# An adaLN transformer block on one core: order of the front loads, of block 1's norm chain and of the last W_o products, with re-chosen plan constants

## The chip, the cores and the metric

The kernel runs on one core of one Trainium2 chip. The metric is device time in microseconds (us); the time before is the median of three runs, 764.05 us (761.28 to 764.38). TensorE multiplies matrices into PSUM (eight banks of 128 x 512 fp32), ScalarE and VectorE read PSUM and write SBUF, GpSimd works on SBUF alone, and transfers are issued from SyncE's queue (SP) and a few from ScalarE's.

## What is computed

One transformer block over 2048 tokens of width 512, 32 heads of 16, hidden width 1376, with the modulation vectors computed from one condition vector c:

```python
mod = (_silu(c) @ w_mod).reshape(c.shape[0], 6, 1, -1)          # sa, ca, ga, sb, cb, gb
h = _layernorm(x) * (1 + ca) + sa
q, k, v = split(h @ wqkv)                                       # 32 heads of 16
o = softmax(q @ k.T * 16 ** -0.5) @ v
x = x + ga * (o @ wo)
h = _layernorm(x) * (1 + cb) + sb
x = x + gb * (gelu(h @ w1 + b1) @ w2 + b2)
```

## The kernel before

Work is cut into four blocks of 512 tokens. Token block b of x lies in tile xb[b]; the normalised and modulated block, transposed, in hT. kT holds the keys, VE the values (with a column of ones per head, which gives the softmax's sum), qm the queries. A *query group* qi (32 of them) is one block of 512 queries with four heads; its 16 key tiles kt hold 128 keys each; a *row* is one head of the four. Scores of a row are one matmul (`qk`, line 807), 128 keys by 512 queries in one bank; the product with the values is one matmul (`pv_issue`, line 963) into O.

Exponentials are made in two ways. ScalarE takes units of two rows (128 x 1024, line 1148, into pA or pB; the two alternate, five buffers each). For some key tiles, named in DKT, VectorE and GpSimd do it: VectorE makes an int16 whose bits, read as a float, approximate a power of two (a *pass*, line 1219, one per row), and then three *shifts* of the whole tile, each an addition of a constant (line 1190 on VectorE, 1196 on GpSimd); these four versions are multiplied with VE and with three scaled copies of it, VV, and their sum is a better exponential. `fill` (line 978) issues matmuls with zeros where TensorE would stand idle.

The **front** (lines 183 to 382) is written in order by hand. c and W_m0 (the first third of w_mod, 1 MB) are loaded from ScalarE's queue; SP issues xb[0] in two halves, then W_k, W_q, xb[1], W_v, xb[2], xb[3], W_m1, and later W_m2 and W_o. VectorE takes `ln_stats` of the four token tiles of xb[0] (line 256), two aggregates after each pair, GpSimd the inverse root (266, 267), VectorE the norm (271); TensorE transposes (275), runs two filler matmuls (`warm`, 234), and then multiplies W_m0 with silu(c) (281), from which hT of block 0 (290 on ScalarE, 293 on VectorE), the first keys and the first queries follow.

From there to the end of attention a **planner** written in Python sets the order. It keeps a clock for each engine (T), asks the engine that is free first what it can do next (`pe`, `act`, `dve`, `pool`), and emits that instruction; the costs it reckons with are constants (EXP_BUSY, PASS_BUSY, the `busy` of each task, `out` as the delay until the result can be used). So a constant changes no instruction by itself, but the order of the instructions on each queue. *Jobs* are matmul groups in a PSUM bank with an evacuation, *tasks* are single instructions on another engine; each has a gate (the position in the list of query groups from which it may be taken) and things that must be done before it. `add_ln1(b)` makes the tasks of the norm of block b: four statistics `st`, an aggregate `ag`, the root `rt` on GpSimd, four norms `nm`, and then transposes (on TensorE for block 1, by DMA for blocks 2 and 3, line 452) and hT; its gate is 0.001 b. `add_k` and `add_v` make the keys (kT, copied at 301 or 303) and the values. Two constants name the part of a gate in which a tail job is spread: U_GATE for the up-projection, OUT_GATE for the down-projection. VectorE's policy is one line:

```python
if o_copy(now) or do_evac(now, DV) or recip(now) or p_pass(now) or do_task(now, DV):
```

so a task is looked at only when no bank waits to be evacuated. GpSimd takes a shift when VectorE has at least POOL_MIN us of open work. The order of the scores is: for key tiles 0 to 3 query groups 0 and 1, then key tiles 4 to 7, and so on for these two groups; from group 2 on, group after group. So ScalarE can do 16 units before it needs the keys of block 1.

After the planner, **`last_tail`** (from line 1410) finishes the last token block by hand: VectorE copies O out (1426), four matmuls pick the sums (1430), VectorE inverts them (1432) and spreads them (1439), four matmuls transpose them (1441), VectorE scales O (1445), and for each of the four token tiles the products with W_o are completed: `outer` adds x and three head groups, `last_ch` the first half of the fourth, the last `plain` (W_z[:, 1]) its second half. Three tiles had their `outer` part as planner jobs; the fourth's stands here. Statistics (1465), norm, transposes, up-projection, gelu, down-projection and the stores follow.

Of the kernel before, what the change touches and what calls it, by code (L numbers as in the profile page):

```python
# [23 lines left out]
D = 512  # L24
# [4 lines left out]
NQB = 4  # L29
# [10 lines left out]
DKT = (3, 7, 11, 13, 14, 15)  # L40
# [10 lines left out]
INF = 1e18  # L51
# [27 lines left out]
U_GATE = (2.0, 4.8)  # L79
# [6 lines left out]
POOL_MIN = 0.9  # L86
# [5 lines left out]
Z_AHEAD = 3  # L92
Z_GATE = 0.35
# [50 lines left out]
def adaln_block(ctx: ExitStack, tc: tile.TileContext, A_x, A_wqkv, A_wo, B_x, B_w1, B_b1, B_w2, B_b2,  # L144
# [28 lines left out]

    def load_mod(i, eng):
        t = prom.tile([P, NC, 2 * D], BF16, name="W_m")
        eng.dma_start(out=t, in_=wm_v[:, :, 2 * i * D:2 * (i + 1) * D])
        return t
# [9 lines left out]
    nc.sync.dma_start(out=W_k, in_=wqkv_v[:, :, D:2 * D])  # L187
    nc.sync.dma_start(out=W_q, in_=wqkv_v[:, :, 0:D])
    nc.sync.dma_start(out=xb[1], in_=x_tok[1])
    nc.sync.dma_start(out=W_v, in_=wqkv_v[:, :, 2 * D:3 * D])  # L190
    for b in range(2, NQB):
        nc.sync.dma_start(out=xb[b], in_=x_tok[b])
    W_m1 = load_mod(1, nc.sync)
# [138 lines left out]

    st0 = small.tile([P, 4, 6], FP32, name="st")
    roots = []
    warm(WARM[0])
    for h in range(2):
        for t in (2 * h, 2 * h + 1):
            ln_stats(xb[0], st0, t)
        mv = ln_aggr(st0[:, 2 * h:2 * h + 2, :], 2)
        roots.append((mv, ln_root(mv, 2)))  # L340
# [10 lines left out]
    norm_pair(0)  # L351
    silu_c()
# [101 lines left out]
    def add_ln1(b):  # L454
# [6 lines left out]
        for t in range(4):  # L461
            task(("st", b, t), g, [("x", b)] + ([("st", b, t - 1)] if t else []), DV, 0.64, lambda t=t: stats(t))
        task(("ag", b), g, [("st", b, 3)], DV, 0.6, lambda: lnst[b].append(ln_aggr(lnst[b][0], 4)))
        task(("rt", b), g, [("ag", b)], PO, 1.35, lambda: lnst[b].append(ln_root(lnst[b][1], 4)))
        for t in range(4):
            task(("nm", b, t), g, [("rt", b)] + ([("nm", b, t - 1)] if t else []), DV, 0.36,
                 lambda t=t: ln_norm(xb[b], xb[b], lnst[b][1], lnst[b][2], t, t))
# [363 lines left out]
    def d_next(now, avoid):  # L831
        if dcur[0] is None:
# [6 lines left out]
            if left < 3:  # L839
                return None  # L840
# [270 lines left out]
    def do_task(now, e):  # L1111
        p = pos()
# [205 lines left out]
    def dve(now):  # L1318
        if o_copy(now) or do_evac(now, DV) or recip(now) or p_pass(now) or do_task(now, DV):
            return True  # L1320
        return hold[0] <= now + 0.03 and emit_shift(DV, now)
# [88 lines left out]
    def last_tail():  # L1410
# [22 lines left out]
        for tt in range(len(pz), 4):  # L1433
            for fn in outer(bank(po[tt]), tt):
                fn()
            last_ch(tt)
# [11 lines left out]
        for tt in range(4):  # L1448
            plain(bank(po[tt]), otl[:, tt * P:(tt + 1) * P], W_z[:, 1, :], False, True)
        warm(12, kw)  # L1450
# [219 lines left out]
```

## Time and profile before

| what | value |
|---|---|
| median of three runs | 764.05 us (761.28 to 764.38) |
| profiled execution: its time / its span | 764.2 us / 762.4 us |
| ScalarE: busy, share of the span | 719.1 us, 94% |
| TensorE: busy, share (fillers included) | 740.0 us, 97% |
| VectorE / GpSimd busy | 689.1 us, 90% / 436.9 us, 57% |
| exponentials on ScalarE | 730 of 128 x 1024, mean 1065 ns |
| VectorE passes / shifts | 588, mean 681 ns / 243, mean 758 ns |
| GpSimd shifts | 198, mean 1898 ns |
| mean granted clock of TensorE | 0.993 |

How to read it: times within the span count from its start. In the timeline a row has the start, the length, engine, line, operation, result and operands, the number of instructions merged into it, and in brackets how long the engine stood idle before it and what released it. Busy times of neighbouring instructions overlap (an exponential takes 1065 ns in the mean, but the next starts some 905 ns after it in an undisturbed run), so the start-to-start distance is what one instruction costs in a full queue. PE is TensorE, PEld its weight load, DVE VectorE, ACT ScalarE, POOL GpSimd.

### The profile page before, as it was taken

Reading aid. Unit: us, or ns where it says so; the run is one execution under the profiler, and the core shown is the slowest. Engines: PE = TensorE matmul, PEld = TensorE weight load, DVE = VectorE, ACT = ScalarE, POOL = GpSimd, SP = SyncE. Lnnn points to the kernel's source line nnn. Section 1 sums busy time; section 2 is a strip of 40 time slices with the busy share of each in tenths; the row PEclk is TensorE's granted clock in tenths of the full one; section 3 lists DMA queues with packets and bytes.
Section 4 is the critical chain, followed back from the end, with each engine's and each line's share of the span. In section 5 each row is a group of like instructions: output and inputs, shape, how many; then the busy total and the mean of one; then the engine's idle time right before and its main releaser. Section 6 shows DMA issues by size and latency. Waiting matters only on the chain.

```text
span 762.4 us, 21212 instructions
## 1 busy us (share of the span) xinstructions
PE 740.0 (97%) x8608; PEld 227.9 (30%) x8608; DVE 689.1 (90%) x1194; ACT 719.1 (94%) x776; POOL 436.9 (57%) x277
## 2 busy tenths in 40 slices
PE   7999999999999999999999999999999999999998
PEld 3322322232222222222222222222232222222255
DVE  5867989999999999999999999999999999999962
ACT  2799999999999999999999999999999999999953
POOL 3201686786568556577558567556667566636610
PEclk9899999999999999999999999999999999999999
DMA  9410100042200200000100200000100200001100
GB/s 314 114 16 2 25 2 18 10 109 67 38 17 3 51 5 16 9 24 24 44 17 3 49 4 17 9 25 24 44 17 10 37 9 17 9 17 30 52 2 31
DMA packets 45969, 25.39 MB, mean 33 GB/s; under 512 B 30973, under 2 KB 40674, under 8 KB 45866
## 3 DMA queue, kind: packets, MB, share of 16 engines
q1 hardware_dynamic: 44906, 22.74, 11.9%
q8 instruction: 69, 1.13, 0.6%
q10 hardware_dynamic: 960, 1.25, 0.5%
q14 instruction: 34, 0.28, 0.1%
HBM read 16.74 MB, written 2.64 MB: 25 GB/s over the span
## 4 chain that ended last, share of the span: by engine, by line
PE 58%; ACT 29%; issue 6%; DVE 4%; DMA 2%; POOL 1%; SPq 1%; ACTq 0%; POOLq 0%; DVEq 0%
PE PS L963 20%; PE PS L807 20%; ACT pB L1148 14%; ACT pA L1148 13%; PE PS L229 13%; PE PS L622 3%; DVE t L1219 2%; DVE t L1190 1%; ACT uG L681 1%; DMA W_m<-in_w_mod_dram 1%; PE PS L978 1%; POOL t L1196 1%; DMA h2T<-uG 0%; SPq L1259 0%; ACT L1148 0%
## 5 line engine op out<-in xcount | busy, mean ns | idle before, releaser
L1196 POOL TENSOR_SCALAR t<-t 128x2048 int16<-128x2048 int16 x198 | 374.2, 1898 | 246.2 <-DVE t L1190 133.6
L1219 DVE TENSOR_SCALAR t<-PS 128x512 int16<-128x512 f32 x588 | 377.5, 681 | 25.8 <-PE PS L807 21.9
L1148 ACT ACTIVATE pA<-PS 128x1024 bf16<-128x1024 f32 x365 | 388.6, 1065 | 4.7 <-PE PS L807 4.4
L1148 ACT ACTIVATE pB<-PS 128x1024 bf16<-128x1024 f32 x365 | 388.9, 1065 | 1.7 <-PE PS L807 0.9
L807 PE MATMUL PS<-qm,kT 32*128 32x512 bf16 x2048 | 303.1, 383 | 6.7 <-ACT pB L1148 2.6
L963 PE MATMUL PS<-t,VV 128*32 128x512 f16 x1764 | 224.5, 384 | 6.2 <-POOL t L1196 3.3
L1190 DVE TENSOR_SCALAR t<-t 128x2048 int16<-128x2048 int16 x243 | 176.5, 758 | 0.5
L807 PEld LDWEIGHTS <-kT 32*128 32x128 bf16 x2048 | 83.9, 91 | 295.8 <-issue 293.9
L963 PE MATMUL PS<-pA,VE 128*32 128x512 bf16 x730 | 169.6, 388 | 0.0
L963 PE MATMUL PS<-pB,VE 128*32 128x512 bf16 x730 | 164.1, 389 | 0.0
L963 PE MATMUL PS<-t,VE 128*32 128x512 f16 x588 | 142.0, 385 | 0.0
L963 PEld LDWEIGHTS <-VE 128*32 128x32 bf16 x2048 | 60.3, 94 | 81.3 <-issue 76.3
L963 PEld LDWEIGHTS <-VV 128*32 128x32 bf16 x1764 | 58.8, 94 | 64.1 <-issue 56.1
L229 PE MATMUL PS<-h2T,W 128*32 128x512 bf16 x528 | 41.7, 383 | 0.9 <-DMA h2T<-uG 0.8
L229 PE MATMUL PS<-W,uG 128*32 128x512 bf16 x528 | 41.5, 383 | 0.0
L978 PE MATMUL PS<-hT,zeros 128*32 128x512 bf16 x360 | 34.4, 387 | 0.0
L1295 POOL TENSOR_TENSOR OT<-o_sb,rb 128x512 bf16<-128x512 f32 x16 | 20.3, 1271 | 12.0 <-DVE t L1190 10.2
L310 DVE TENSOR_SCALAR qm<-PS,qmask 128x512 bf16<-128x512 f32 x32 | 22.7, 741 | 3.7 <-PE PS L229 3.4
L673 DVE TENSOR_SCALAR uG<-PS,b1c 128x512 bf16<-128x512 f32 x33 | 24.5, 743 | 1.5 <-PE PS L229 1.2
L266 POOL TENSOR_SCALAR rs<-mv 128x4 f32<-128x4 f32 (+1 forms) x10 | 4.3, 431 | 31.6 <-DVE mv L261 31.2
L229 PE MATMUL PS<-hT,W_k 128*32 128x512 bf16 x256 | 21.4, 410 | 0.9 <-DVE hT L293 0.9
L229 PE MATMUL PS<-hT,W_q 128*32 128x512 bf16 x256 | 21.6, 399 | 0.0
(128 smaller groups left out, 377.8 us busy)
## 6 DMA issues: line engine op xcount, KB each, us to landing
rb<-d SPq DMA_DIRECT2D x120, 32.0 KB
W_m<-in_w_mod_dram SPq DMA_DIRECT2D x2, 1024.0 KB
xr<-in_A_x_dram SPq DMA_DIRECT2D x4, 512.0 KB
o_sb<-o SPq DMA_DIRECT2D x60, 32.0 KB
out_dram<-ob SPq DMA_DIRECT2D x14, 128.0 KB
xb<-in_A_x_dram SPq DMA_DIRECT2D x3, 512.0 KB
W<-in_B_w_dram SPq DMA_DIRECT2D x4, 344.0 KB
W<-in_B_w_dram SPq DMA_DIRECT2D x5, 256.0 KB
```

The costliest lines, as they stand in the source:

```text
L229: nc.tensor.matmul(out=ps[32 * g:32 * g + 32, :], lhsT=lhsT[:, 32 * g:32 * g + 32], rhs=rhs, start=start, stop=stop)
L310: nc.vector.tensor_scalar(out=qm[(b, ch)][:, par, :], in0=ps, scalar1=qmask[:, par:par + 1], scalar2=None, op0=ALU.mult)
L622: nc.tensor.matmul(out=ps, lhsT=lhsT, rhs=rhs, start=start, stop=stop)
L673: nc.vector.tensor_scalar(out=X["u"][:, fc, :], in0=bank(ps), scalar1=late["b1c"][:, fc:fc + 1], scalar2=None, op0=ALU.add)
L807: nc.tensor.matmul(out=dst, lhsT=kT[32 * r:32 * r + 32, ch, kt * P:(kt + 1) * P], rhs=qm[(b, ch)][32 * r:32 * r + 32, par, :], start=True, ...
L963: nc.tensor.matmul(out=bank(O[qi])[32 * r:32 * r + 32, :], lhsT=w, rhs=rhs, start=(n == 1), stop=last)
L978: nc.tensor.matmul(out=bank(O[qi])[32 * r:32 * r + 32, :], lhsT=zeros[:, 0:32], rhs=hT[:, r, 0:512], start=False, stop=False)
L1148: nc.scalar.activation(out=t[:, 0:n, :], in_=PS[:, b0:b0 + n, :], func=ACT.Exp, scale=math.log(2.0) / STEP)
L1190: nc.vector.tensor_scalar(out=t16[:, rs, :], in0=d["tile"][:, rs, :], scalar1=float(MJ[j]), scalar2=None, op0=ALU.add)
L1196: nc.gpsimd.tensor_scalar(out=t16[:, rs, :], in0=d["tile"][:, rs, :], scalar1=1.0, scalar2=float(MJ[j]), op0=ALU.mult, op1=ALU.add)
L1219: nc.vector.tensor_scalar(out=d["tile"][:, r:r + n, :], in0=PS[:, i:i + n, :], scalar1=T_BIAS, scalar2=0.0, op0=ALU.add, op1=ALU.max)
L1295: nc.gpsimd.tensor_tensor(out=ot, in0=o, in1=rb, op=ALU.mult)
```

## The change

Front loads: W_k, W_q, xb[1], W_v, xb[2] and xb[3] are put in a list. After the first statistic of xb[0], W_k is issued with a dependency on that VectorE instruction, and W_q behind it; after the fourth, xb[1] with a dependency on it, and the others behind it. W_m1 is issued after the first `norm_pair`. Block 1's chain: while fewer than 32 score tiles are taken, VectorE looks first for a task with a gate up to 0.0015, that is, block 1's statistics, aggregate and norms. The plan's cost of a statistic is 0.61 instead of 0.64, and statistics and norms have no delay (`out=0.0`). The last tail: the last products of tiles 0 and 1 now stand ahead of the fourth tile's `outer` and `last_ch`, those of tiles 2 and 3 behind them, and ten fillers follow instead of twelve. Four constants are others; D_END only names the 3 that stood in the code.

```diff
@@ -37,7 +37,7 @@
 TURNS = {}
 TURN = 2
-DKT = (3, 7, 11, 13, 14, 15)
+DKT = (2, 3, 7, 13, 14, 15)
 NV = 4
 STEP = 1024.0
@@ -76,20 +76,22 @@
 K_GATE = (-1.8, 0.4)
 Q_GATE = -0.9
 X1_GATE = (0.3, 1.3)
-U_GATE = (2.0, 4.8)
+U_GATE = (1.7, 5.0)
 OUT_GATE = (4.6, 7.8)
 OPEN_N = 12
 DMA_T = 4.0
 LN1_DMA = (2, 3)
 LN2_DMA = True
 D_PEND = 3
-POOL_MIN = 0.9
+POOL_MIN = 1.0
 D_WAIT = 0.6
 WHY = False
 TIE = True
 SEARCH = None
 NARROW = False
 Z_AHEAD = 3
+LOAD_AT = (0, 3)
+D_END = 3
 Z_GATE = 0.35
@@ -171,6 +173,18 @@
     wqkv_v = A_wqkv.rearrange("(j p) n -> p j n", p=P)
     wo_v = A_wo.rearrange("(c p) n -> p c n", p=P)
+    def load_next(dst, src, after=None):
+        n0 = len(nc.cur_bb.bb.instructions)
+        nc.sync.dma_start(out=dst, in_=src)
+        if after is not None:
+            mine = [i for i in nc.cur_bb.bb.instructions[n0:] if i.engine == nc.sync.engine]
+            tc.add_manual_dep(mine[0], after.name,
+                              mybir.DependencyInfo(mybir.DependencyClass.Sync, mybir.DependencyReason.DATA),
+                              reason="turn")
+
+    def last_dve():
+        return [i for i in nc.cur_bb.bb.instructions if i.engine == nc.vector.engine][-1]
+
     def load_mod(i, eng):
         t = prom.tile([P, NC, 2 * D], BF16, name="W_m")
         eng.dma_start(out=t, in_=wm_v[:, :, 2 * i * D:2 * (i + 1) * D])
@@ -184,13 +198,6 @@
     for t in range(0, 4, 2):
         nc.sync.dma_start(out=xb[0][:, t:t + 2, :], in_=x_tok[0][:, t:t + 2, :])
     W_m0 = load_mod(0, nc.scalar)
-    nc.sync.dma_start(out=W_k, in_=wqkv_v[:, :, D:2 * D])
-    nc.sync.dma_start(out=W_q, in_=wqkv_v[:, :, 0:D])
-    nc.sync.dma_start(out=xb[1], in_=x_tok[1])
-    nc.sync.dma_start(out=W_v, in_=wqkv_v[:, :, 2 * D:3 * D])
-    for b in range(2, NQB):
-        nc.sync.dma_start(out=xb[b], in_=x_tok[b])
-    W_m1 = load_mod(1, nc.sync)
     ident = const.tile([P, P], BF16, name="ident")
     make_identity(nc, ident)
@@ -330,12 +337,21 @@
         nc.vector.tensor_scalar(out=heads(VV[:, DKT.index(kt), j - 1, :]), in0=heads(VE[:, kt, :]),
                                 scalar1=WJ[j], scalar2=None, op0=ALU.mult)
+    loads = deque([(W_k, wqkv_v[:, :, D:2 * D]), (W_q, wqkv_v[:, :, 0:D]), (xb[1], x_tok[1]),
+                   (W_v, wqkv_v[:, :, 2 * D:3 * D]), (xb[2], x_tok[2]), (xb[3], x_tok[3])])
     st0 = small.tile([P, 4, 6], FP32, name="st")
     roots = []
     warm(WARM[0])
     for h in range(2):
         for t in (2 * h, 2 * h + 1):
             ln_stats(xb[0], st0, t)
+            if t == LOAD_AT[0]:
+                load_next(*loads.popleft(), last_dve())
+                load_next(*loads.popleft())
+            if t == LOAD_AT[1]:
+                load_next(*loads.popleft(), last_dve())
+                while loads:
+                    load_next(*loads.popleft())
         mv = ln_aggr(st0[:, 2 * h:2 * h + 2, :], 2)
         roots.append((mv, ln_root(mv, 2)))
     ident32 = const.tile([P, P], FP32, name="ident32")
@@ -349,6 +365,7 @@
                 transpose_one(bank16(j), xb[0], j, 2 * h + i, 2 * h + i)
     norm_pair(0)
+    W_m1 = load_mod(1, nc.sync)
     silu_c()
     norm_pair(1)
     warm(WARM[1])
@@ -459,12 +476,12 @@
         g = 0.001 * b
         for t in range(4):
-            task(("st", b, t), g, [("x", b)] + ([("st", b, t - 1)] if t else []), DV, 0.64, lambda t=t: stats(t))
+            task(("st", b, t), g, [("x", b)] + ([("st", b, t - 1)] if t else []), DV, 0.61, lambda t=t: stats(t), out=0.0)
         task(("ag", b), g, [("st", b, 3)], DV, 0.6, lambda: lnst[b].append(ln_aggr(lnst[b][0], 4)))
         task(("rt", b), g, [("ag", b)], PO, 1.35, lambda: lnst[b].append(ln_root(lnst[b][1], 4)))
         for t in range(4):
             task(("nm", b, t), g, [("rt", b)] + ([("nm", b, t - 1)] if t else []), DV, 0.36,
-                 lambda t=t: ln_norm(xb[b], xb[b], lnst[b][1], lnst[b][2], t, t))
+                 lambda t=t: ln_norm(xb[b], xb[b], lnst[b][1], lnst[b][2], t, t), out=0.0)
         if b in LN1_DMA:
             for t in range(4):
                 task(("ht", b, t), g, [("nm", b, t)], "SP", 0.0,
@@ -836,7 +853,7 @@
             if aq < D_FROM - 1 or done.get(("h", NQB - 1), INF) > now:
                 return None
             left = sum(1 for i in range(st["ap"], len(order)) if order[i] not in owner) if aq >= NQ - 1 else 99
-            if left < 3:
+            if left < D_END:
                 return None
             for i in range(st["ap"], min(len(order), st["ap"] + 32)):
                 qi, kt = order[i]
@@ -1108,8 +1125,8 @@
                 return True
         return False
-    def do_task(now, e):
-        p = pos()
+    def do_task(now, e, upto=INF):
+        p = min(pos(), upto)
         for tk in tasks:
             if tk.gate > p:
                 break
@@ -1316,6 +1333,8 @@
         return True
     def dve(now):
+        if st["ap"] < 32 and do_task(now, DV, 0.0015):
+            return True
         if o_copy(now) or do_evac(now, DV) or recip(now) or p_pass(now) or do_task(now, DV):
             return True
         return hold[0] <= now + 0.03 and emit_shift(DV, now)
@@ -1430,10 +1449,6 @@
             nc.tensor.matmul(out=bank(kd)[:, 4 * tt:4 * tt + 4], lhsT=o[:, tt * P:(tt + 1) * P], rhs=pick,
                              start=True, stop=True)
         nc.vector.reciprocal(out=rt.rearrange("p t r -> p (t r)"), in_=bank(kd)[:, 0:16])
-        for tt in range(len(pz), 4):
-            for fn in outer(bank(po[tt]), tt):
-                fn()
-            last_ch(tt)
         for tt in range(4):
             cs = slice(tt * P, (tt + 1) * P)
             nc.vector.tensor_copy(out=rx[:, cs].rearrange("p (r e) -> p r e", e=32),
@@ -1445,9 +1460,18 @@
             nc.vector.tensor_tensor(out=otl[:, cs], in0=o[:, cs], in1=bank(kr)[:, cs], op=ALU.mult)
         nc.sync.dma_start(out=scr_d1, in_=o.rearrange("(r e) n -> r e n", e=32)[:, 14, :])
         nc.sync.dma_start(out=dall[:, NQ - 1, :], in_=scr_d1.rearrange("r (p f) -> (r p) f", f=16))
-        for tt in range(4):
+        def last_par(tt):
             plain(bank(po[tt]), otl[:, tt * P:(tt + 1) * P], W_z[:, 1, :], False, True)
-        warm(12, kw)
+
+        for tt in range(2):
+            last_par(tt)
+        for tt in range(len(pz), 4):
+            for fn in outer(bank(po[tt]), tt):
+                fn()
+            last_ch(tt)
+        for tt in range(2, 4):
+            last_par(tt)
+        warm(10, kw)
         def up_one(fc, cs, k):
             ps = bank(k)[:, 0:256]
```

## The prediction

> **What bounds the kernel now.** I read the page first, then ScalarE's waits, then ScalarE's instructions in order of time, then the two ends of the span. Engine shares of the page:
>
> ```profile
> PE 740.0 (97%) x8608; PEld 227.9 (30%) x8608; DVE 689.1 (90%) x1194; ACT 719.1 (94%) x776; POOL 436.9 (57%) x277
> L1148 ACT ACTIVATE pA<-PS 128x1024 bf16<-128x1024 f32 x365 | 388.6, 1065 | 4.7 <-PE PS L807 4.4
> L978 PE MATMUL PS<-hT,zeros 128*32 128x512 bf16 x360 | 34.4, 387 | 0.0
> ```
>
> TensorE's 97% is not its limit: 360 of its matmuls (90 groups of four) multiply zeros to fill idle time. ScalarE's exponentials wait 4.7 us in all, so between its first and last one the span is ScalarE's, except where it stands still. Its instructions around the only long stop:
>
> ```profile
> 30.89 1.08 ACT L1148 ACTIVATE pB<-PS 128x1024 bf16<-128x1024 f32 x1
> 33.20 0.78 ACT L290 ACTIVATE hT<-PS,modc 128x512 bf16<-128x512 bf16 x1 [1.23 <-PE PS L275]
> 36.33 0.59 ACT L301 CAST kT<-PS 128x512 bf16<-128x512 f32 x1 [2.34 <-PE PS L229]
> 37.81 1.02 ACT L1148 ACTIVATE pA<-PS 128x1024 bf16<-128x1024 f32 x1 [0.90 <-PE PS L807]
> ```
>
> The 16 exponentials of key block 0 end at 31.97; the 17th starts at 37.81. The 5.84 us between are block 1's chain (statistics, norm, transposes, hT, W_k, kT copy) coming late. Three stretches of one clock window each (columns: PE, PEld, DVE, ACT, POOL busy, then granted clock, DMA share, GB/s):
>
> ```profile
> 23.00:26.43 3.43, 3.40 (x40) 0.94 (x37) 3.43 (x7) 3.43 (x5) 1.26 (x2) 1.00 0.05 16
> 26.43:29.84 3.41, 2.73 (x25) 1.32 (x24) 3.30 (x12) 3.41 (x5) 1.34 (x2) 1.00 0.03 7
> 29.84:33.25 3.41, 3.34 (x29) 1.23 (x30) 3.17 (x13) 2.18 (x4) 0.74 (x1) 0.50 0.40 77
> ```
>
> VectorE is full until 31 us, so the order of its queue decides when block 1's chain ends; and TensorE, short of work at 26 to 30 us, then has half its clock until 36.7. The front and the end of attention, from the timeline:
>
> ```profile
> 9.19 0.59 PE L234 MATMUL PS<-zeros 128*128 128x512 bf16 x2
> 10.58 0.95 PE L281 MATMUL PS<-sc_bf,W_m 128*128 128x1 bf16 x32 [0.80 <-DMA W_m<-in_w_mod_dram]
> ...
> 723.96 4.58 DVE L1190 TENSOR_SCALAR t<-t 128x2048 int16<-128x2048 int16 x5
> ...
> 724.86 1.14 ACT L1148 ACTIVATE pB<-PS 128x1024 bf16<-128x1024 f32 x1
> ...
> 728.11 1.04 PE L963 MATMUL PS<-t,VV 128*32 128x512 f16 x16
> ...
> 729.20 0.69 DVE L1426 COPY o_sb<-PS 128x512 f32<-128x512 f32 x1 [0.66 <-PE PS L963]
> ```
>
> TensorE waits 0.80 us for W_m. ScalarE ends at 726.00, but the last copy of O starts 3.2 us later: five shifts on VectorE and their products are last there.
>
> **Front loads.** No transfer is added; W_k waits for the first BN statistics (4.02 + 0.64 = 4.66), xb[1] for the fourth (6.69). Queued behind them on SP are only W_q, W_v, xb[2], xb[3], W_m1, W_m2 and W_o, in the old order. By the windows of 2 us DMA moves 265, 378 and 368 GB/s from 2 to 8 us, that is 0.53, 1.29 and 2.02 MB by 4, 6 and 8 us. xb[0] and W_m0 are 1.5 MB: if nothing else is in flight, W_m0 is there by about 6.7 instead of 10.58. What is late next is TensorE's own order: its two fillers end at 9.78, so the gain is 10.58 - 9.78 = **0.8 us**. W_k and W_q make 2.5 MB, so by 9.5 us or, should the queue run dry for a moment, 10; they are needed at 11.6 and 13.1. W_v and xb[1] make 3.5 MB, 12.3 us, and are needed at 14.9 and 16.5. The cover is 2 to 3 us; without it each us late costs one. Bounds: a gain of 0.8, and nothing if W_m0 still trails.
>
> **Block 1's chain.** The instruction orders of the two programs, side by side, show VectorE after the two qm products (next start 17.28 before): 4 statistics, aggregate, 2 V copies, 1 statistic, 4 norms, 2 V copies, then 4 statistics, a kT copy and an aggregate between hT 0 to 3. Ahead of hT 3 are 9 statistics and 5 copies at 0.60 start to start (17.28 to 19.06; 19.06 to 19.65), 2 aggregates at 0.28 (22.63 to 22.91), 4 norms at 0.32 (25.27 to 25.59), 3 hT at 0.46 (29.11 to 29.57): 8.40 + 0.56 + 1.28 + 1.38 = 11.62, so hT 3 starts at 28.90 and ends at 29.44, where ScalarE ended it at 33.98 before. The root on GpSimd takes 1.8 us from the aggregate (22.63 to 24.43), 19.68 to 21.48, and the norms stand at 21.76: hidden. TensorE's order puts half of W_k's 16 matmuls behind the 16th pair's scores (30.18), then 16 W_v matmuls and 8 products, then the 17th pair's scores. At full clock 16 such matmuls take 0.86, 8 take 0.43: 30.5 + 0.43 + 0.86 + 0.43 + 0.1 = 32.3, and the exponential follows 0.48 later (37.33 to 37.81), at 32.8. VectorE's kT copy (after 4 norms and a statistic, at 31.24, end 31.9) is hidden. At half clock 16 take 1.70 (34.35 to 36.05): 30.5 + 0.86 + 1.7 + 0.7 = 33.8, exponential at 34.3. So the stop shrinks by **5.0 or 3.5 us**. The changed TensorE has in 26.4 to 29.8 four score pairs, 12 products and 6 to 8 transposes and no fillers, about what the half-clock row above had: I take 3.5.
>
> The Trainium skill (TensorE: Matmul & The Clock Gate, Part 1) says that the clock halves after at least one idle window of about 3.4 us. The trace differs: the window 26.43 to 29.84 had TensorE busy 2.73 of 3.41 us and the clock still was 0.50 in the next. By the Trainium skill's rule no window of the changed kernel is idle here, and the sum would take 5.0.
>
> What is late next: block 2's kT. Its norms end at 30.8, its four DMA transposes are issued every 1.22 us and land about 4 us after the last issue (38.9 to the wait that ends at 43.04), so at 37.6; four hT and nine other VectorE steps later kT is there at about 44. It is needed 16 units after 34.3, at 49. VectorE may stand at hT for some 3 us from 34.7, with V copies behind it; ScalarE's ten probability buffers cover that.
>
> **Plan constants.** The side-by-side orders give counts: exponentials 730 to 732, VectorE passes 588 to 584, shifts on VectorE 243 to 245 and on GpSimd 198 to 193, filler matmuls 360 to 300. Only ScalarE's matter: (726.00 - 37.81 - 3 x (4.90 + 2 x 1.28) for the gelus) / 714 = 0.933 us each, two make **+1.9**. VectorE changes by -4 x 0.60 + 2 x 0.73 = -0.9 and GpSimd by -5 x 1.9 off the bound. Gelu gates, other tiles in DKT and cost figures move work between queues at equal counts; the trace bounds them by the jitter of ScalarE's starts after the 17th: they lie 16 us in sum above 0.905 each (gelus left out); a quarter of it, 4 us either way, I keep for the range and take 0.
>
> At the end the order now has seven score pairs behind the last one with VectorE rows (before two): ScalarE ends 3.67 + 5 x 0.905 = 8.2 us after it. VectorE has about 1.6 of passes, a reciprocal of 0.25 and six shifts at 0.92 (4.58 / 5) after it, 7.4: done before ScalarE. So O's copy follows ScalarE by one product (0.38) and its hand-overs, 0.7, not 3.2: **-2.5**. Bounds: nothing gained, and -2.7.
>
> **W_o products.** Before, five matmuls for the fourth tile (issued until 731.93) hold the 1/sum transposes back although VectorE's first copy is done at 731.6: moved behind, 0.3 is gained. They then stand ahead of the third tile's last product: 733.24 + 2 x 0.21 + 5 x 0.21 + 0.4 = 735.1, while VectorE reaches that tile's statistics at 735.1 as well instead of 735.36. **-0.2**; bounds -0.3 to +0.3. Two fillers fewer hide behind the norm.
>
> **Sum**, against the profiled 764.2 (span 762.4; the median of the three runs is 764.05): -0.8 - 3.5 + 1.9 - 2.5 - 0.2 = -5.1, so **759.1 us**.
>
> **Rivals.**
> The clock stays full: 5.0 for 3.5, and in front W_k and W_q run at full clock too (now 0.50 from 12.77 to 16.18; about 1.0 of W_q): 756.6. For it: the front's quiet window has 0.8 more work. Against: the row above. It is what the Trainium skill's rule of the idle window would give. Chance 0.20.
> The end does not drain faster, because VectorE's shifts run late (0.92 each beside a busy GpSimd): -0.8 - 3.5 + 1.9 - 0.2, 761.6. Chance 0.19.
> The chain does not come earlier, because V copies behind the norms hold TensorE's banks: the stop stays; -0.8 + 1.9 - 2.5 - 0.2, 762.6. Against: those copies slip by under 1 us. Chance 0.11.
> Slower: the new order makes scores late for ScalarE all through the middle (VectorE at 90% shifts more itself, two more there, five fewer on GpSimd). Each ns of mean pitch costs 0.716 us; at +7 ns the gain is gone, from 0.945 us on (+12.4) it is slower by over 0.5%; at +15 ns 769.8. Chance 0.12.
> The forecast has 0.38. 0.5% is 3.8 us, about what a measurement of this kernel can tell from no change: below 760.4 is faster. Forecast and first rival carry most of faster, with a part of the forecast above the bound: 0.56; same 0.32; slower 0.12. Range 755.5 to 765.0, from the first rival's -1 to the fourth rival's beginning and the jitter on the two between.
>
> **What would show it.** The W_m wait gone and its matmuls at about 9.8; the 17th exponential at 33.5 (34.3 - 0.8); the granted clock in 29 to 33 us; the mean pitch of the exponentials still 0.93; the last copy of O within 1 us of the last exponential; the second pair of statistics in the tail starting 5.95 us after that copy (6.16 before). The prediction is wrong if the pitch grows, or if the stop only moves to block 2 (a wait of ScalarE near 48 us).

## The result, and the profile after

The changed kernel takes **768.34 us** (median of 15 runs, 764.09 to 770.29) against 762.01 us (15 runs, 761.04 to 766.84) of the kernel before: a ratio of 1.0066 with an interval of 1.0048 to 1.0085. It is slower, where a faster kernel with 759.1 us was forecast, and it lies outside the range of 755.5 to 765.0. The profiled execution of it took 769.9 us (span 768.1), that of before 764.2 (span 762.4).

The engine shares, the exponentials and the fillers of the page after (each group: busy time, mean ns of one, then the idle time before them and what ended most of it):

```profile
PE 745.6 (97%) x8534; PEld 225.0 (29%) x8534; DVE 686.2 (89%) x1193; ACT 721.9 (94%) x777; POOL 427.5 (56%) x272
L1165 ACT ACTIVATE pA<-PS 128x1024 bf16<-128x1024 f32 x366 | 387.4, 1058 | 8.6 <-PE PS L824 8.1
L1165 ACT ACTIVATE pB<-PS 128x1024 bf16<-128x1024 f32 x366 | 387.5, 1059 | 7.1 <-PE PS L824 6.3
L995 PE MATMUL PS<-hT,zeros 128*32 128x512 bf16 x300 | 29.8, 389 | 0.0
```

The counts are those of the forecast (732 exponentials, 300 fillers), and one exponential costs what it did (1058 ns in the mean, before 1065). What is new is that ScalarE waits 14.4 us for scores, where it waited 5.3. The start of block 1 on ScalarE, from the timeline after:

```profile
29.20 1.19 ACT L1165 ACTIVATE pB<-PS 128x1024 bf16<-128x1024 f32 x1
30.46 0.59 ACT L308 CAST VE<-PS 128x512 bf16<-128x512 f32 x1
31.27 1.02 ACT L1165 ACTIVATE pA<-PS 128x1024 bf16<-128x1024 f32 x1 [0.22 <-PE PS L824]
```

The stop ahead of the 17th exponential is gone: 16th to 17th start take 2.07 us, before 6.92. The windows of that stretch, and the front and the end of attention:

```profile
26.43:29.84 3.41, 3.21 (x45) 1.19 (x46) 3.21 (x9) 3.41 (x5) 0.79 (x1) 1.00 0.19 38
29.84:33.25 3.41, 3.41 (x54) 1.14 (x47) 2.99 (x10) 3.12 (x5) 1.25 (x2) 1.00 0.44 85
```

```profile
9.66 0.94 PE L288 MATMUL PS<-sc_bf,W_m 128*128 128x1 bf16 x32
...
732.18 1.08 ACT L1165 ACTIVATE pB<-PS 128x1024 bf16<-128x1024 f32 x1
...
734.72 0.69 DVE L1445 COPY o_sb<-PS 128x512 f32<-128x512 f32 x1 [4.85 <-PE PS L980]
```

The clock stays full (1.00), W_m is no longer waited for, and O's last copy comes 1.46 us after the last exponential ends (3.20 before). So front, block 1 and the end of attention moved the way they should. To see where the time went I put the start of each exponential beside that of the same number before:

| exponential | before | after | difference |
|---|---|---|---|
| 16th | 30.89 | 29.20 | -1.69 |
| 17th | 37.81 | 31.27 | -6.54 |
| 65th | 83.33 | 75.79 | -7.54 |
| 75th | 92.58 | 88.03 | -4.55 |
| 160th | 172.67 | 167.80 | -4.87 |
| 175th | 186.42 | 186.79 | +0.37 |
| 190th | 200.23 | 200.35 | +0.12 |
| 200th | 209.27 | 215.00 | +5.73 |
| 220th | 227.82 | 233.26 | +5.44 |
| 730th | 724.86 | 730.30 | +5.44 |

From the 220th to the 730th both kernels take 497.04 us. All of the loss falls in three places before 215 us: 3.0 us at 77 to 84, 5.2 us at 172 to 184, 5.6 us at 202 to 210. The last two are stops of ScalarE. What ends its long waits is a score of TensorE; what TensorE waits for is a shift of VectorE; and what VectorE waits for is this (timeline after):

```profile
172.37 0.25 DVE L1288 RECIPROCAL rp<-dall 128x16 f32<-128x16 f32 x1 [1.91 <-DMA dall<-d]
...
173.22 0.61 PE L980 MATMUL PS<-t,VV 128*32 128x512 f16 x2 [1.56 <-DVE t L1207]
...
174.54 1.02 ACT L1165 ACTIVATE pA<-PS 128x1024 bf16<-128x1024 f32 x1 [2.02 <-PE PS L824]
...
201.50 0.25 DVE L1288 RECIPROCAL rp<-dall 128x16 f32<-128x16 f32 x1 [3.52 <-DMA dall<-d]
...
203.81 1.22 PE L980 MATMUL PS<-t,VV 128*32 128x512 f16 x6 [2.37 <-DVE t L1207]
...
205.67 1.02 ACT L1165 ACTIVATE pB<-PS 128x1024 bf16<-128x1024 f32 x1 [3.16 <-PE PS L824]
```

The softmax sums of a query group go through DRAM: d<-o or d<-o_sb writes them, dall<-d reads them back in another layout, and VectorE inverts them (line 1271, 1288 after). The reciprocal stands in VectorE's queue; when its dall is not there, every pass and shift behind it waits too. SP's queue of the second of these groups, after and then before:

```profile
193.12 0.48 SPq L1273 DMA_DIRECT2D d<-o_sb  x1
...
194.18 0.48 SPq L604 DMA_DIRECT2D b<-o  x1
...
195.93 3.14 SPq L616 DMA_DIRECT2D b1p<-b  x4
...
199.12 0.68 SPq L1279 DMA_DIRECT2D dall<-d  x1
```

```profile
188.00 0.48 SPq L1256 DMA_DIRECT2D d<-o_sb  x1
189.66 0.35 SPq L1262 DMA_DIRECT2D dall<-d  x1
192.77 0.50 SPq L587 DMA_DIRECT2D b<-o  x1
194.55 3.06 SPq L599 DMA_DIRECT2D b1p<-b  x4
```

In the plan made anew, the bias write b<-o and the four bias reads b1p<-b stand ahead of the read of dall: it starts 6.00 us after the write of the sums, before 1.66. The group at 172 us, after and then before:

```profile
164.80 0.53 SPq L1273 DMA_DIRECT2D d<-o  x1
...
167.88 1.10 SPq L567 DMA_DIRECT2D W<-in_B_w_dram  x2
169.08 0.41 SPq L1279 DMA_DIRECT2D dall<-d  x1
```

```profile
167.62 0.53 SPq L1256 DMA_DIRECT2D d<-o  x1
...
170.70 0.58 SPq L550 DMA_DIRECT2D W<-in_B_w_dram  x1
171.38 0.41 SPq L1262 DMA_DIRECT2D dall<-d  x1
```

Here two W_2 loads stand ahead of it, before one: it starts 4.28 us after the write against 3.76. The larger part of this wait is that the reciprocal stands earlier in VectorE's queue: it starts 3.29 us after the issue of its read and has waited for it, where before it started 3.08 us after (174.46) without a wait.

The planner could not see either. Its clocks T are four, for TensorE, ScalarE, VectorE and GpSimd; a transfer on SP is put at a time of the plan, its issue costs nothing there, and a small one like these is taken to be done 2.2 us later (the constant DMA). In the trace the four bias reads alone hold SP for 3.14 us.

Behind each stop the clock falls. Windows after (PE, PEld, DVE, ACT, POOL busy, then granted clock, DMA share, GB/s):

```profile
169.50:172.97 3.47, 2.16 (x18) 0.53 (x15) 1.56 (x4) 3.02 (x4) 0.66 (x1) 1.00 0.68 218
172.97:183.20 10.23, 9.98 (x65) 1.73 (x64) 6.63 (x12) 6.19 (x7) 5.77 (x4) 0.50 0.15 42
200.00:203.70 3.70, 1.44 (x12) 0.36 (x11) 2.20 (x6) 2.51 (x3) 0.00 (x0) 1.00 0.23 6
203.70:210.50 6.80, 6.69 (x49) 1.19 (x48) 5.05 (x9) 3.36 (x4) 3.18 (x3) 0.50 0.34 96
```

TensorE was idle for 1.3 and 2.3 us of the windows ahead of these, and then has half its clock for 10.2 and 6.8 us, in which ScalarE (6.19 of 10.23 and 3.36 of 6.80 us busy) is fed too slowly.

### The profile page after: what moved, and what is told of

Read it like the earlier page. It is cut to its first block, busy times and chain, and to the rows that moved or that the text cites. A ratio compares the mean times of both kernels' runs of the same rounds, so it can differ in the third digit from the quotient of the medians.

```text
span 768.1 us, 21071 instructions
## 1 busy us (share of the span) xinstructions
PE 745.6 (97%) x8534; PEld 225.0 (29%) x8534; DVE 686.2 (89%) x1193; ACT 721.9 (94%) x777; POOL 427.5 (56%) x272
## 4 chain that ended last, share of the span: by engine, by line
PE 58%; ACT 24%; DVE 7%; issue 5%; DMA 3%; SPq 2%; POOL 1%; DVEq 0%; POOLq 0%
PE PS L980 21%; PE PS L824 20%; PE PS L236 12%; ACT pB L1165 11%; ACT pA L1165 11%; PE PS L639 3%; DVE t L1236 2%; DVE t L1207 2%; DMA dall<-d 1%; ACT uG L698 1%; POOL t L1213 1%; DMA W_v<-in_A_wqkv_dram 1%; PE PS L995 1%; SPq L1276 1%; DVE qm L317 1%
## 5 line engine op out<-in xcount | busy, mean ns | idle before, releaser
L1213 POOL TENSOR_SCALAR t<-t 128x2048 int16<-128x2048 int16 x193 | 365.7, 1901 | 244.5 <-DVE t L1207 133.5
L1165 ACT ACTIVATE pA<-PS 128x1024 bf16<-128x1024 f32 x366 | 387.4, 1058 | 8.6 <-PE PS L824 8.1
L824 PE MATMUL PS<-qm,kT 32*128 32x512 bf16 x2048 | 309.7, 387 | 4.9 <-ACT pB L1165 2.3
L980 PE MATMUL PS<-t,VV 128*32 128x512 f16 x1752 | 227.9, 391 | 7.6 <-DVE t L1207 4.6
L1207 DVE TENSOR_SCALAR t<-t 128x2048 int16<-128x2048 int16 x245 | 179.1, 756 | 0.0
L980 PE MATMUL PS<-pB,VE 128*32 128x512 bf16 x732 | 166.6, 390 | 0.0
L980 PE MATMUL PS<-t,VE 128*32 128x512 f16 x584 | 149.1, 389 | 0.3 <-DVE t L1236 0.3
L236 PE MATMUL PS<-h2T,W 128*32 128x512 bf16 x528 | 43.6, 383 | 0.2 <-DVE t L1236 0.2
L995 PE MATMUL PS<-hT,zeros 128*32 128x512 bf16 x300 | 29.8, 389 | 0.0
L633 POOL TENSOR_TENSOR W<-W,gbk 128x512 bf16<-128x512 bf16 x11 | 12.7, 1156 | 16.4 <-DVE t L1207 13.2
```

Of the source, the lines that this page charges most:

```text
L236: nc.tensor.matmul(out=ps[32 * g:32 * g + 32, :], lhsT=lhsT[:, 32 * g:32 * g + 32], rhs=rhs, start=start, stop=stop)
L824: nc.tensor.matmul(out=dst, lhsT=kT[32 * r:32 * r + 32, ch, kt * P:(kt + 1) * P], rhs=qm[(b, ch)][32 * r:32 * r + 32, par, :], start=True, ...
L980: nc.tensor.matmul(out=bank(O[qi])[32 * r:32 * r + 32, :], lhsT=w, rhs=rhs, start=(n == 1), stop=last)
L995: nc.tensor.matmul(out=bank(O[qi])[32 * r:32 * r + 32, :], lhsT=zeros[:, 0:32], rhs=hT[:, r, 0:512], start=False, stop=False)
L1165: nc.scalar.activation(out=t[:, 0:n, :], in_=PS[:, b0:b0 + n, :], func=ACT.Exp, scale=math.log(2.0) / STEP)
L1207: nc.vector.tensor_scalar(out=t16[:, rs, :], in0=d["tile"][:, rs, :], scalar1=float(MJ[j]), scalar2=None, op0=ALU.add)
```

## The experiments

**Theory**: SP's order in the new plan makes dall late twice; the wait runs from VectorE through TensorE to ScalarE, and the half clock behind each stop adds about as much again. **Rivals**: the other constants (tiles in DKT, gelu gates) load VectorE or put scores late everywhere; or the front and the tail lose what block 1 gains.

### One part alone: front loads and tail

The change without the planner's edits; every order between front and tail is that of before.

```diff
-DKT = (2, 3, 7, 13, 14, 15)
+DKT = (3, 7, 11, 13, 14, 15)
-U_GATE = (1.7, 5.0)
+U_GATE = (2.0, 4.8)
-POOL_MIN = 1.0
+POOL_MIN = 0.9
...
-        if st["ap"] < 32 and do_task(now, DV, 0.0015):
-            return True
```

(and 0.64 and the delays of the norm's tasks again)

> The kernel before with the front loads and the W_o products of the change alone; the plan of the middle is instruction for instruction that of before. Theory (the loss sits in the re-made plan: on SP weight loads and the reads of b1p now stand ahead of the read of the softmax sums, dall, and VectorE's reciprocal waits for it in its queue): the W_m wait of 0.8 us goes, the tail gives 0.1; about 1 us faster than before, 761, reciprocals waiting for dall about 1 us in all as before, stop before the 17th exponential still about 5 to 6 us. Rival (the gated front loads come late or push later transfers): 765 or more, with waits for W_v, xb or W_q in the profile.

762.58 us (12 runs), ratio 1.0013 [0.9998, 1.0028]: no gain, where about 1 us was expected. A likely reason shows when the front's W_m matmuls are compared over all profiles: with the old loads they wait for W_m in three of five executions (0.80, 0.98, 0.96 us; in the two others they start at 9.49 and 9.68 without a wait), with the new loads in none of eight (9.64 to 9.75). So only some executions have that microsecond to gain; that the times show none is not explained by this alone. And here the 17th exponential starts 4.38 us after the 16th with the order of before at full clock (a stop of 3.2 us, where about 5 to 6 was expected); 6.92 was that order at half clock.

### Only SP's order: dall first

In the code, `later(dt, f)` puts an issue off by dt us of the plan's time.

```diff
-            later(10.0 + 2.0 * i, lambda i=i: nc.sync.dma_start(out=W_2[:, 2 * i:2 * i + 2, :],
+            later(12.5 + 2.0 * i, lambda i=i: nc.sync.dma_start(out=W_2[:, 2 * i:2 * i + 2, :],
...
-            nc.sync.dma_start(out=late["b1p"][:, r, :], in_=scr_b[r:r + 1, :].rearrange("o (f p) -> p (o f)", p=P))
+            later(3.0, lambda r=r: nc.sync.dma_start(
+                out=late["b1p"][:, r, :], in_=scr_b[r:r + 1, :].rearrange("o (f p) -> p (o f)", p=P)))
```

> The changed kernel, whose order is kept on TensorE, VectorE, ScalarE and GpSimd; only on SP the four b1p reads are issued behind the dall read next to them, and the W_2 loads 2.5 us of plan time later, so that one of them instead of two stands ahead of the other dall read. Theory: the two stops of ScalarE near 172 and 201 us (2.0 and 3.2 us of waiting, 10.5 us with the half clock behind them) go; 768.3 - 10.5 = 758, reciprocals waiting for dall under 2 us. Rival (the half clock comes from the free-running window and a plan with fewer fillers, not from these stops): waits go, but stretches at half clock stay as long as they are, about 24 us, and the time stays above 763.

760.22 us (12 runs), ratio to before 0.9975 [0.9961, 0.9989], from the change's 1.0066: SP's order alone is worth 0.9%, some 7 us, a little less than expected (758). The order of instructions on VectorE, ScalarE and GpSimd is the same in both traces. SP's queue in this run (the timeline), and VectorE's and ScalarE's waits (us in all, times, longest):

```profile
187.96 0.35 SPq L1280 DMA_DIRECT2D dall<-d  x1
189.09 3.34 SPq L616 DMA_DIRECT2D b1p<-b  x4
```

```profile
DVE rp L1289 <- DMA dall<-d: 3.1, 5, 1.1
ACT pA L1166 <- PE PS L825: 2.7, 4, 1.5
ACT pB L1166 <- PE PS L825: 0.9, 2, 0.7
```

Both stops are gone: the difference to before is -7.79 us at the 160th exponential, -6.86 at the 190th, -6.91 at the 730th, and the clock is full until the tail. The reciprocal of the first group still waits 1.06 us. A few rows on a queue with little to do decide the sign of the change. It beats both kernels and is the best version found.

### Half of it: only the bias reads late

The second hunk of the diff above alone.

> The changed kernel with the four b1p reads behind the dall read, and nothing else. Theory: the stop near 201 us goes and the one near 172 stays: 768.3 - 5.3 = 763. Rival (half clock from the window alone): above 765.

762.37 us (12 runs), ratio 1.0006 [0.9991, 1.0022]. The stop at 202 us is gone; the other stays, with a reciprocal that waits 1.92 us, half clock from 172.7 to 179.5 us, and 4.1 us lost from the 160th to the 175th exponential. So each of the two stops is its own, and each has its own row on SP.

### The old constants

DKT, U_GATE and POOL_MIN of before in the changed kernel.

> The changed kernel with DKT, U_GATE and POOL_MIN of before; front, block 1's priority, its cost figures and the tail as changed. On SP one W_2 load instead of two stands between O's rows and dall, as before, but the b1p reads stand ahead of the next pair of transfers for dall. Theory (order of SP decides): the stop near 172 goes, one near 200 may stay; 757 to 763. Rival (block 1 earlier is itself what hurts): 767 or more.

764.44 us (12 runs), ratio 1.004 [1.0019, 1.006], above what was expected. The two stops are not there (reciprocals wait 0.7 us in all), but the profiled execution has one of its own:

```profile
602.53 1.05 PE L236 MATMUL PS<-h2T,W 128*32 128x512 bf16 x8 [1.73 <-DMA h2T<-uG]
...
604.22 1.02 ACT L1165 ACTIVATE pA<-PS 128x1024 bf16<-128x1024 f32 x1 [2.30 <-PE PS L824]
```

TensorE waits for a DMA transpose, and the clock is halved from 602.0 to 608.9 us. The exponentials go from -3.98 us at the 600th to -0.48 at the 650th, and there are 734 of them. So the two stops belong to the plan that comes of the new values, but the values need no stop: dall first keeps them and has none. Each plan made anew has waits at other places.

### A late dall in the kernel before

Small reads into a spare tile ahead of the read of dall; no other engine's order changes. Ten in groups 6 and 18, then sixteen in groups 5 and 6:

```diff
+            if qi in (5, 6):
+                for n in range(16):
+                    nc.sync.dma_start(out=late["idle"][:, n, :], in_=d1.rearrange("r (p f) -> (r p) f", f=16))
             nc.sync.dma_start(out=dall[:, qi, :], in_=d1.rearrange("r (p f) -> (r p) f", f=16))
```

> The kernel before, with ten reads of 128x16 from a DRAM tensor into a spare tile put on SP just ahead of the read of dall in query groups 6 and 18; no other engine's order changes, and nothing of the change is in it. At about 0.45 us for one issue the read of dall starts some 4.5 us later in these two groups. Theory (an SP row that stands ahead of the read of dall holds VectorE's reciprocal, behind it the shifts, behind those TensorE's products, and so ScalarE's exponentials): the reciprocal in order waits 2 to 4 us in both groups, ScalarE stops twice for scores, each stop leaves 2 to 5 us in the times of the exponentials behind it with the half clock that follows, and the time is 0.5 to 1.2 % above before (ratio 1.004 to 1.012). Rival (what costs the time in the kernel after is its other order or the load on VectorE, and late reads of dall are hidden by the reserve of scores): ratio 0.998 to 1.002.

Ten: 762.89 us (12 runs), ratio 1.0012 [0.9991, 1.0032], and the theory's number missed. Group 6's reciprocal waited 1.40 us, group 18's (at 460.36 us) not at all, and the exponentials lost 0.1 us over the one that did: here the scores and probabilities in reserve cover it.

> The kernel before with sixteen small reads into a spare tile on SP just ahead of the read of dall, in the query groups 5 and 6; every other engine's order is as before. Ten such reads took 4.62 us and made the reciprocal of group 6 wait 1.40 us, which cost nothing that could be measured; sixteen take 7.4 us, so that reciprocal waits about 4.2 us, and that of group 5, which stood closer to its dall, 4 to 6. Theory (a reserve of scores covers the first 1.5 us or so, what is beyond it stops ScalarE and TensorE, and the clock may halve behind the stop): two waits of ScalarE for scores of 2 to 5 us each, ratio 1.004 to 1.013. Rival (a late dall is covered, and the loss of the change comes from elsewhere in its plan): ratio 0.998 to 1.002.

Sixteen: 776.69 us (6 runs), ratio 1.0167 [1.0129, 1.0206], more than expected. VectorE and ScalarE in the timeline:

```profile
180.32 0.25 DVE L1274 RECIPROCAL rp<-dall 128x16 f32<-128x16 f32 x1 [7.21 <-DMA dall<-d]
205.57 0.25 DVE L1274 RECIPROCAL rp<-dall 128x16 f32<-128x16 f32 x1 [4.08 <-DMA dall<-d]
```

```profile
182.46 1.02 ACT L1148 ACTIVATE pB<-PS 128x1024 bf16<-128x1024 f32 x1 [7.41 <-PE PS L807]
...
210.30 1.02 ACT L1148 ACTIVATE pB<-PS 128x1024 bf16<-128x1024 f32 x1 [2.98 <-PE PS L807]
```

With nothing of the change in it, a late dall stops the kernel before in the same way. Over the runs, the wait of one reciprocal and what the exponentials lose around it:

| run | wait | lost | clock behind it |
|---|---|---|---|
| before, ten reads, group 6 | 1.40 | 0.1 | full |
| dall first, group 5 | 1.06 | 0.8 | full |
| norm's cost figures alone (below), group 5 | 1.19 | 1.4 | full |
| the same, group 1 | 2.53 | 2.2 | full |
| changed kernel, group 5 | 1.91 | 5.2 | half for 10.2 us |
| bias reads late, group 5 | 1.92 | 4.1 | half for 6.8 us |
| changed kernel, group 6 | 3.52 | 5.6 | half for 6.8 us |
| before, sixteen reads, group 6 | 4.08 | 5.9 | half for 10.2 us |
| before, sixteen reads, group 5 | 7.21 | 8.3 | half for 6.8 us |

With the clock full behind it, a wait costs 0.1 to 2.2 us, at most about its own length; with half clock behind it, 1.1 to 3.3 us more than its length. A fixed reserve does not show: 1.40 us cost 0.1 in one place, 1.19 us cost 1.4 in another.

### The half clock by itself

The changed kernel with matmuls by zeros on TensorE (adding nothing) where the two reciprocals stand in the plan, to keep it busy in the stops; only TensorE's order differs. 28 and 40 of them, then 28 and 80:

```diff
+            if qi in (5, 6) and all(emitted[qo][r] and emitted[qo][r] != total(qo) for r in range(4)):
+                for _ in range({5: 7, 6: 20}[qi]):
+                    for r in range(4):
+                        nc.tensor.matmul(out=bank(O[qo])[32 * r:32 * r + 32, :], lhsT=zeros[:, 0:32],
+                                         rhs=hT[:, r, 0:512], start=False, stop=False)
```

> The kernel after, with 28 and 40 more matmuls by zeros on TensorE where the reciprocals of the two query groups with the late dall are planned (adding zeros to sums), so that TensorE is busy longer in the two stops; only TensorE's order differs. Theory that the stop itself is half of the loss and the half clock behind it the other half: the two waits of ScalarE for scores stay at 2 to 3 us each, the clock is not halved at 173 and 204 us, and the time is 763 to 766 us, 2.5 to 5 us below after (ratio to before 1.001 to 1.006). Rival (the clock has no part, the exponentials are late by the stop alone): the time of after, ratio 1.006 to 1.008, with the clock full or not.

With 40: 768.58 us (6 runs), ratio 1.0082 [1.0056, 1.0107]; the time is the rival's, not the theory's. The 40 ended before the second stop began, and the clock halved there as before, so the time decides nothing. The first stop is the test that worked (windows of this run):

```profile
172.00:175.00 3.00, 3.00 (x46) 0.99 (x45) 1.21 (x4) 1.91 (x3) 0.21 (x1) 1.00 0.49 140
175.00:184.00 9.00, 8.77 (x88) 2.77 (x85) 8.53 (x15) 8.72 (x11) 6.90 (x5) 1.00 0.18 46
```

The reciprocal waits as long (1.79 us), the clock stays full, and the exponentials lose 1.5 us from the 160th to the 175th in place of 5.2.

> As fill_stops, with 80 in place of 40 matmuls by zeros at the second stop, where 40 ended before the stop began. Theory (the half clock behind a stop is a consequence of TensorE's idleness and costs about as much as the stop): the clock stays full in 196 to 215 us, the exponentials lose 2 to 3.5 us over the second stop instead of 4.9 to 5.6, and the median is 764 to 767 us. Rival: the loss over the second stop stays at 5 us or more with the clock full.

With 80: 765.64 us (12 runs), ratio 1.0028 [1.0007, 1.0050]. The clock is full through both stops (windows):

```profile
170.50:173.50 3.00, 2.86 (x36) 0.79 (x29) 1.97 (x4) 1.52 (x2) 1.26 (x1) 1.00 0.33 89
196.00:199.00 3.00, 3.00 (x51) 1.15 (x40) 0.37 (x2) 0.15 (x1) 0.00 (x0) 1.00 0.19 9
```

The first costs 1.7 us. The second lies between the two expectations, for the 80 matmuls (4.50 us) themselves stand ahead of scores: ScalarE waits 3.71 us behind them, and the 175th to the 200th exponential lose 4.7 us. The reciprocal there waits longer, too (5.11 us, in the changed kernel 3.52). Both stops together take 6.4 us where the changed kernel has 10.6 (its -4.87 to +5.73): about 4 us of it were the clock.

### The kernel before once more

> The kernel before once more, unchanged, for a second profile of it. Theory that the profile the forecast was read from was one with more half clock than most executions: the stop in block 1 ahead of the 17th exponential is 3.3 to 4.5 us instead of 5.84, and the span is 757 to 761 us. Rival: 5.5 to 6 us again in any profile, with the clock halved there. Ratio 0.999 to 1.001.

762.57 us (12 runs), ratio 1.0002 [0.9984, 1.0019]. The stop in block 1 was 5.52 us (31.28 to 36.80), with half clock, as the rival said. But it is not so in any profile: four with this order have 6.92, 6.54, 5.48 and 4.28 us from the 16th to the 17th start, with half clock in that stretch for 6.8, 6.8, 3.4 and 0 us. The profile that the forecast was read from is the one with the longest stop.

### What brought block 1 forward

The changed kernel without the priority line in VectorE's planner:

> The kernel after without the one line of VectorE's planner that puts block 1's norm chain ahead of evictions (the constants stay new, so the plan is made anew again). Theory: the stop ahead of the 17th exponential comes back (3 to 5 us), the exponentials start 16 to 17 in the order of before; whether dall comes late depends on where SP's loads fall in this plan: in its order the reads of dall in group 5 stand behind one W_2 load only and those of group 6 ahead of the bias reads, so the two stops at 172 and 203 us are gone. Then 761 to 765 us, ratio 1.000 to 1.004. Rival (the priority line does nothing and the front loads alone brought the 17th exponential forward): the 17th exponential starts at 31 to 33 us, and the time is 757 to 760.

762.37 us (12 runs), ratio 1.0008 [0.9984, 1.0032]; ScalarE's timeline:

```profile
28.78 1.09 ACT L1165 ACTIVATE pB<-PS 128x1024 bf16<-128x1024 f32 x1
29.68 0.67 ACT L308 CAST kT<-PS 128x512 bf16<-128x512 f32 x1
30.96 1.02 ACT L1165 ACTIVATE pA<-PS 128x1024 bf16<-128x1024 f32 x1 [0.61 <-PE PS L824]
```

The stop did not come back: the 17th follows 2.18 us after the 16th. So the line is not needed for it. The time lies in the theory's range by luck, for its mechanism failed; and this plan has 734 exponentials, two more than the changed kernel. The kernel before with nothing but the norm tasks' cost figures:

```diff
-            ... DV, 0.64, lambda t=t: stats(t))
+            ... DV, 0.61, lambda t=t: stats(t), out=0.0)
-                 lambda t=t: ln_norm(xb[b], xb[b], lnst[b][1], lnst[b][2], t, t))
+                 lambda t=t: ln_norm(xb[b], xb[b], lnst[b][1], lnst[b][2], t, t), out=0.0)
```

> The kernel before with only the cost figures of the norm chain as in the change (0.61 and no result latency for statistics and norms); front loads, priority line, constants and tail are those of before. Theory after the run without the priority line (these two figures alone bring block 1's chain forward): the 17th exponential starts within 2.5 us of the end of the 16th, at 31 to 33.5 us, and the time is 757 to 761 us, ratio 0.994 to 0.999, less what a late dall costs in group 5, where this plan puts two W_2 reads ahead of it. Rival (it was the constants): the 17th at 35 us or later, ratio 0.999 to 1.002.

The 17th exponential starts 2.18 us after the 16th (28.52 and 30.70): these two figures alone are enough to move the chain. The time was missed, 768.61 us (11 runs), ratio 1.0063 [1.0038, 1.0088]. This plan, too, has late reads (reciprocals wait 2.53 us at 85 and 1.19 at 172 us) and loses 2.2 and 1.4 us over them; it loses 3.2 more from 181 to 189 us, with half clock for 3.4 us and no wait for dall, and it has 734 exponentials, four more than before.

### All runs by their clock

Time goes with the mean granted clock of the execution (correlation 0.80 over the 97 runs of the kernel before in these experiments). A straight line through them gives 760.9 us at clock 1.0 and 0.51 us more for each 0.001 less; the slopes of the other runs' kernels lie between 0.33 and 0.71.

| kernel | mean clock of its runs | median at 0.991 to 0.993 (runs) |
|---|---|---|
| before | 0.9968 | 763.9 (19) |
| changed | 0.9882 | 765.5 (4) |
| dall first | 0.9955 | 761.1 (4) |
| bias reads late | 0.9927 | 762.2 (8) |

At equal clock the changed kernel is only 1.6 us slower; of its 6.3 us the lower clock has the rest, 4.7 (0.0086 less at 0.51 us per 0.001 gives 4.4). And dall first is 2.8 us faster at equal clock. Two cautions: the changed kernel and dall first have four runs each in that band, the highest clocks of the one and the lowest of the other; and the lower clock is in part the work of the change itself, by its stops, so the comparison splits the loss and does not take it off the change.

## Why the prediction was wrong

By its own steps, profile after against profile before:

| step | forecast | measured |
|---|---|---|
| front loads | -0.8 | -0.92 at W_m's matmuls (-1.69 at the 16th exponential) |
| block 1's stop | -3.5 (5.0 if the clock stays full) | -4.85 (6.92 to 2.07) |
| two more exponentials | +1.9 | +1.88 |
| end of attention | -2.5 | -1.74 |
| W_o products | -0.2 | -0.07 (second statistics 6.09 after O's copy, before 6.16) |
| plan constants, order after the 17th | 0, 4 either way | +12.0 (-6.54 at the 17th to +5.44 at the 730th) |

Of the 12.0 us the two stops are 10.8, the half clock at 77 us is 3.0, and the rest, -1.8, lies in the stretches between, -1.0 of it from the 17th to the 65th exponential.

**The step that failed** is the one that put the rest of the new plan at nothing: "Gelu gates, other tiles in DKT and cost figures move work between queues at equal counts; ... a quarter of it, 4 us either way, I keep for the range and take 0." Equal counts said nothing of the order on SP, to which the planner gives no clock. I had counted ScalarE's, VectorE's and GpSimd's instructions, read SP's order in the front alone, and asked "what is late next" of block 2's keys, where no wait came. The reads of dall, each with a VectorE instruction in order behind it, I did not look at. The waits that resulted are shown by undoing SP's order alone (1.0066 to 0.9975) and by making dall late in the kernel before (1.0167). The bound of 4 us, taken from the scatter of starts within one plan, could not hold what a stop costs in another plan. (The scatter was also misread: the starts lie 18.7 us in sum above 0.905 each, not 16, which makes the quarter 4.7.)

**The half clock was in the forecast at one place, in block 1, where it went the right way.** That a new stop would bring it elsewhere was not priced. TensorE waits 1.56 and 2.37 us, and its clock is then half for 10.2 and 6.8; filling the first stop took it from 5.2 to 1.5 us.

**Block 1** gave more than forecast; the clock stayed full in 26 to 33 us, with TensorE busy 3.21 of 3.41 us where I had expected about 2.7. That rival was right on its own term. Of the 4.85 us about 2.2 are the order (4.28 and 4.38 to 2.07, all at full clock) and the rest the half clock that it avoids, which not every execution of before has. So without the half clock the other terms are worth -0.9 - 2.2 + 1.9 - 1.7 - 0.1 = -3.0 us. Dall first, which has them without the two stops, is 2.8 us faster than before at equal clock and 1.4 by the medians over all runs (760.22 against 761.63): the forecast's -5.1 counted half clock that one profile of before had and others have less of or not at all.

**The end**: the last products and O's copy follow ScalarE by 1.46 us, not 0.7: 16 products of the last shifts were still to do after the last exponential began (732.98 and 733.64), where one was counted. So the second rival (no faster end) fell, and so did the third (the stop stays).

**The fourth rival** (scores late through the middle, VectorE loaded more) was right in its sign and fell as a mechanism: 220th to 730th exponential take the same 497.04 us in both kernels. That its 769.8 us for 15 ns more of mean pitch lies beside the profiled 769.9 is luck: from the 17th to the 730th the mean pitch did grow by 16.8 ns, from 963.6 to 980.4, but by the stops ahead of the 220th, not by a slower middle.

What stays open: the 3.0 us at 77 to 84 us of the changed kernel. The clock was halved there without a stop. Of the five profiles with this order up to there, those with 40 and 80 fillers lose 3.0 and 1.6 us in the same place, dall first and bias reads late lose nothing. It comes and goes between executions. A count at the end of this document points to small matmuls and to where a clock window falls on them; no experiment was made on it. Nor is it known why the transfer of group 5's sums takes longer (3.29 us from the issue of its read to the reciprocal, in group 6 2.38).

## What to carry to other kernels

When constants of a planner change, every queue is a new one: compare the order on the transfer queue too, and for each small read that an in-order engine waits for, look at what now stands between its write and itself. If the planner has no clock for a queue, the plan cannot show a wait on it. A stop is priced at up to its own length, and then at the half clock behind it if TensorE runs dry; measure what a reserve covers at the place itself (here 1.40 us cost 0.1 at one and 1.19 us cost 1.4 at another) before saying that a late read is hidden. And look at the granted clock of each execution before a few us of one profile are put down to an edit, asking whether the edit itself lowered it.

## What the runs showed of the hardware

The stretches of half clock are 3.41, 6.83 or 10.24 us long in all profiles (but for the one that the end of the span cuts), multiples of one window, and fall at other places of the same program in other executions: 28.44 in the second profile of before, 29.84 in the first. Within one profile their starts lie on one grid: in that of the changed kernel 172.99 and 203.71 us are 28 and 37 windows behind 77.42. The Trainium skill (TensorE: Matmul & The Clock Gate, Part 1) has the window at 3413 ns and free-running, and the traces agree. It has the clock fall after at least one idle window; here it also fell after windows in which TensorE was busy 2.16 of 3.47 us and 1.44 of 3.70, and once, at 77.4 us, after one with hardly a gap (windows after):

```profile
74.00:77.40 3.40, 3.36 (x53) 1.72 (x47) 3.40 (x6) 3.40 (x5) 3.27 (x2) 1.00 0.03 5
77.40:84.20 6.80, 6.80 (x54) 1.34 (x58) 3.98 (x10) 4.47 (x6) 3.12 (x2) 0.50 0.11 24
```

That window holds the 32 matmuls with W_m2 (line 288, one column each). They keep TensorE busy in the trace and add next to no work, and a count of work separates the windows better than busy time does. Take each matmul by its columns and its share of the array, in units of one with 512 columns on a quarter of it (as a score matmul is), on each trace's own grid of windows. The 13 traces have 2709 windows at full clock before 720 us, with 41 units in the median. All 13 with fewer than 18.2 units are followed by half clock, 8 of the 33 with 18.2 to 23.1, and none of the 2663 with more. The window with the 32 small matmuls has 16.8, 17.7 and 18.3 units in the three executions that lose time there, 21.6 and 24.7 in the two that do not, because their grid lies elsewhere. This is a count over the traces as they are; no run was made to test it.
